# Two-layer kernel on one core: the gate's product ahead of the step's relu, a high part moved from step 10 to step 8 of a segment, and stage B's sums taken through PSUM

## The chip, the cores and the metric

The kernel runs on one core of one Trainium2 chip. The time is device microseconds of one execution, given as the median of several. Besides that, one execution was taken by the hardware profiler; all views below come from it. Engines: PE is TensorE (matmul), DVE is VectorE, ACT is ScalarE, POOL is GpSimd, SP issues the DMAs.

## The reference

The input x has 4 batches of 12608 tokens with 128 channels. First an induced attention with 32 inducing points, then a channel mix with 1024 hidden channels:

```python
def mab(q, kv):
    s = scale * (q @ kv.transpose(0, 2, 1))
    a = np.exp(s - s.max(-1, keepdims=True))
    a /= a.sum(-1, keepdims=True) + 1e-09
    return a @ kv
h = mab(I, x)                 # I: 32 inducing points
x = mab(x, h)                 # every token attends to the 32 rows of h
x_prev = x shifted by one token
xk = mu_k * x + (1.0 - mu_k) * x_prev
xr = mu_r * x + (1.0 - mu_r) * x_prev
k = np.maximum(xk @ w_k, 0.0)
v = k * k @ w_v
r = 1.0 / (1.0 + np.exp(-(xr @ w_r)))
out = r * v
```

## The kernel before

Channels lie on the partitions, tokens in the free dimension. A batch is cut into 25 groups of 512 tokens (the last has 320), and a group's 1024 hidden channels into 4 units of 256. One unit is one **step**; there are 400 steps, numbered n, and every step issues the same skeleton:

- `up`: four matmuls of 512 columns into the PSUM tile `ps_a` (two buffers; lines 773 and 775). The weights W hold h times w_k, so that the second attention's product is folded into them, and R holds the attention weights as a high and a low part.
- `square`: the **relu** on DVE, `ps_a` to `k_t` (line 785); then `kh`, the square rounded to float32r (**high part**), by ACT from `k_t` (line 790) or, in the steps that the set `high_vector` names, by DVE from `ps_a` (line 787); then ACT's full square in place in `k_t` (line 791); then POOL's difference `kl` = `k_t` - `kh` (line 793). `k_t`, `kh` and `kl` have four buffers each.
- in a group's second step, `zgate`: two matmuls (lines 762 and 763) into the bank `ps_v` (two buffers) for the group, and ACT's sigmoid into `rT` (line 765).
- `down` of the step four before: six matmuls (line 804) that sum into the group's `ps_v`.
- one step after a group's last `down`, the **gate**: `oT` = `ps_v` times `rT` on DVE (line 809). It frees the bank that the `zgate` of the next step takes. A step later `store` transposes `oT` into `ot` (line 820), and every fourth group four DMAs write `ot` out.

Beside this run two other stages, put into the steps by numbers written out by hand (`at`: at the end of a step; `soon`: after its `up`). They repeat every 12 steps, a **segment**; steps 0 to 11 below count within it, and the gate falls into steps 0, 4 and 8.

- **Stage A** (of the next batch, so in batches 0 to 2, six segments each): the first attention over a block of 2048 tokens. Step 9 ends with its scores on PE (line 361, into bank a of `pb`) and DVE's maximum (line 364); step 11 has the small matmul `common` (line 371) into bank b of `pb`, and DVE's running maximum; in a batch's last segment `t_scores` (line 349) goes into bank b in step 11 as well. The sum over tokens goes into bank a (line 426), from where `acc` on DVE takes it in step 8 (line 441).
- **Stage B** (all batches): the second attention's weights for a block. Step 1 ends with its scores on PE into bank b (line 610); then on DVE a transpose and the maximum (lines 617, 620), the subtraction (line 623) in step 3, ACT's exponential in step 4, in step 6 the sums over 32 points, the added 1e-9 and the reciprocal (lines 631, 632, 635), in step 7 the product and the transpose back into bank b. ACT copies a rounded high part `ah` in step 8 (line 650), DVE takes the **low part** `al` in step 10 (line 654), which is the last reader of bank b. SP then spreads both into R.

The program keeps the order in which it is written on each engine; each engine runs its own list in order and waits at semaphores.

Of the kernel before, what the change touches and what calls it, by code (L numbers as in the profile page):

```python
# [8 lines left out]
F32 = mybir.dt.float32  # L9
# [4 lines left out]
ALU = mybir.AluOpType  # L14
AX = mybir.AxisListType
EPS = 1e-9
# [3 lines left out]
def kernel(  # L20
# [11 lines left out]
    nc = tc.nc  # L32
# [3 lines left out]
    P = 128  # L36
    Q = 4
# [7 lines left out]
    LAG = 4  # L45
    NU = FC // UC
# [8 lines left out]
    sm = ctx.enter_context(tc.tile_pool(name="sm", bufs=2))  # L55
# [7 lines left out]
    def pb_tile(bank=None):  # L63

        return pb.tile([P, G], F32, name="pb_" + (bank or next(banks)))
# [516 lines left out]
    def halo(S, g, far=True):  # L582

        if g == 0:
            nc.vector.memset(S.R[g].bitcast(F32)[:, 0:1], 0.0)
        elif far:
            nc.sync.dma_start(out=S.R[g].bitcast(F32)[:, 0:1], in_=S.R[g - 1].bitcast(F32)[:, G:G + 1])
        else:
            nc.vector.tensor_copy(out=S.R[g][:, 0:1], in_=S.R[g - 1].bitcast(F32)[:, G:G + 1])


    def stage_b(b, j, at, t):

        S = batches[b]
        full = j < NBLK - 1
        L = {}
        if full:
            w = G  # L600
        else:
            w = (TAIL // Q + 31) // 32 * 32
            offs = [min(i * w, TAIL - w) for i in range(Q)]
        nk = w // 32

        def scores():
            ps = L["ps"] = pb_tile("b")
            for i in range(Q):
                rhs = S.xt[j, i] if full else S.xt_tail[:, offs[i]:offs[i] + w]
                nc.tensor.matmul(out=ps[M * i:M * (i + 1), :w], lhsT=S.hT, rhs=rhs,  # L610
                                 start=True, stop=True)
            for i in range(Q):
                S.xt.pop((j, i))

        def trans():
            L["s2"] = st.tile([P, Q * Q, M], F32, name="s2")[:, :nk, :]
            nc.vector.transpose(out=L["s2"].rearrange("p k m -> p (k m)"), in_=L["ps"][:, :w])

        def maxi():
            nc.vector.tensor_reduce(out=L["ps"][:, :nk], in_=L["s2"], op=ALU.max, axis=AX.X)  # L620

        def sub():
            nc.vector.tensor_tensor(out=L["s2"], in0=L["s2"], op=ALU.subtract,
                                    in1=L["ps"][:, :nk].unsqueeze(2).broadcast_to([P, nk, M]))

        def expo():
            nc.scalar.activation(out=L["s2"], in_=L["s2"], func=AF.Exp, scale=scale)

        def total():
            L["sm"] = sm.tile([P, Q * Q, 2], F32, name="sm3", bufs=1)[:, :nk, 0]  # L630
            nc.vector.tensor_reduce(out=L["sm"], in_=L["s2"], op=ALU.add, axis=AX.X)
            nc.vector.tensor_scalar(out=L["sm"], in0=L["sm"], scalar1=EPS, scalar2=None, op0=ALU.add)  # L632

        def recip():
            nc.vector.reciprocal(out=L["ps"][:, :nk], in_=L["sm"])

        def mult():
            nc.vector.tensor_tensor(out=L["s2"], in0=L["s2"], op=ALU.mult,
                                    in1=L["ps"][:, :nk].unsqueeze(2).broadcast_to([P, nk, M]))

        def back():
            L["aT"] = L["ps"][:, :w]
            if full and b > 0:
                nc.vector.transpose(out=L["aT"].rearrange("p (q s) -> p s q", q=M), in_=L["s2"])
            else:
                nc.vector.transpose(out=L["aT"], in_=L["s2"].rearrange("p k m -> p (k m)"))

        def high():
            L["ah"] = st.tile([P, G], F32R, name="ah")[:, :w]
            nc.scalar.copy(out=L["ah"], in_=L["aT"])  # L650

        def low():
            L["al"] = st.tile([P, G], F32R, name="al")[:, :w]
            nc.vector.tensor_tensor(out=L["al"], in0=L["aT"], in1=L["ah"].bitcast(F32), op=ALU.subtract)

        def spread(i):
            src = (L["ah"].bitcast(F32), L["al"].bitcast(F32))
            if full or i == 0:
                S.R[j * Q + i] = r_pool.tile([P, G + 1], F32R, name="R")
                halo(S, j * Q + i)  # L660
            R = S.R[j * Q + (i if full else 0)].bitcast(F32)
            o, lo = (0, 0) if full else (offs[i], i * w - offs[i])
            for q in range(Q):
                nc.sync.dma_start(out=R[M * q:M * (q + 1), 1 + o + lo:1 + o + w],  # L664
                                  in_=src[q % 2][M * i:M * (i + 1), lo:w])

        at(t, scores)
        at(t + 1, trans)
        at(t + 1, maxi)
        at(t + 2, sub)  # L670
        at(t + 3, expo)
        at(t + 5, total)
        at(t + 5, recip)
        at(t + 6, mult)
        at(t + 6, back)
        at(t + 7, high)
        at(t + 9, low)
        for i in range(Q):
            at(t + 10 + i, lambda i=i: spread(i))
# [154 lines left out]
    def run(th):  # L834
        for f in th:
            f()
# [58 lines left out]
    def head():  # L895


        last = NBLK - 1
        for k in range(2):
            ab[k].tr()  # L900
        ab[0].scores()
        for k in range(NBLK):
            ab[k].maxi()
            ab[k].expo()
            place(PARTS[k][0])
            if k > 0:
                ab[k - 1].hmm()
            if k == last:
                maxes()
            if k > 0:  # L910
                ab[k - 1].acc()
            if k == 0:
                constants()
            if k + 2 < NBLK:
                ab[k + 2].tr()
            place(PARTS[k][1])
            ab[k].etrans()
            ab[k].ecopy()
            ab[k].sums()
            if k < last:  # L920
                ab[k + 1].scores()
            place(PARTS[k][2])
        spin(8)
        weights()
        ab[last].hmm()
        place(PARTS_END)
        ab[last].acc()
        load_x(1, 0)
        hfin()
        place(len(work))  # L930
# [5 lines left out]
    def at(n, f):  # L936
        events.setdefault(n, []).append(f)
# [43 lines left out]
    high_vector = set()  # L981
    for b in range(B):
        t = b * UB + (4 if b == 0 else 0)
        for j in range(NBLK - 1):
            s = t + SEG * j
            high_vector |= {s + 4, s + 10}
            if b + 1 < B:
                stage_a(b + 1, j, at, s)
            stage_b(b, j + 1, at, s + 1)
        if b + 1 < B:  # L990
            s = t + SEG * (NBLK - 1)
            combine(b + 1, at, s)
            stage_b(b + 1, 0, at, s + 13)
    units = []
# [6 lines left out]
    with tc.manual_schedule():  # L1001
        head()
        start()
        for n in range(len(units) + LAG + 2):
            grp, u = units[n] if n < len(units) else (None, n % NU)
            old, ou = units[n - LAG] if LAG <= n < len(units) + LAG else (None, 0)
            if grp is None:
                run(late)
                late = []
            else:  # L1010
                grp.up(u)
                run(early.pop(n, []))
                low = grp.square(u, n in high_vector)
                run(late)
                late = []
                part = grp.w - (grp.w // 2 if n >= len(units) - 3 else 0)
                low(nc.gpsimd, 0, part)
                if part < grp.w:
                    late = [lambda low=low, a=part, z=grp.w: low(nc.vector, a, z)]
                if n == end:  # L1020
                    run(late)
                    late = []
                if n >= NU and u == 1:
                    grp.zgate()
                if u == NU - 2 and n + 2 < len(units):
                    nxt = units[n + 2][0]
                    if nxt.b == 0 and nxt.g < Q:
                        halo(nxt.S, nxt.g, far=False)
            m = n - LAG - 1
            if 0 <= m < len(units) and units[m][1] == NU - 1:  # L1030
                units[m][0].gate()
            if 1 <= m <= len(units) and units[m - 1][1] == NU - 1:
                units[m - 1][0].store()
            if old is not None:
                old.down(ou)
            run(events.pop(n, []))
# [30 lines left out]
```

## Time and profile before

| | before |
|---|---|
| median of 3 runs | 1220.78 us (1220.38 to 1222.27) |
| the profiled execution's own time | 1221.54 us |
| its span, first to last instruction | 1219.7 us |
| PE, DVE, ACT, POOL busy | 92%, 79%, 80%, 78% |
| granted TensorE clock, mean | 0.994 |

Rows of the timeline read: start in us, length in us, engine, line, operation, output<-inputs with their shapes, count, and in brackets the idle time of the engine just before it and what ended it. Rows of waits read: engine, what it wanted to start, whom it waited for, then total us, times, longest us. Rows by line and form read: total busy us, mean ns of one, then idle time before. Rows by windows read: the stretch, its length, then busy us and instruction count of PE, of PE's weight loads, of DVE, ACT and POOL, then the granted clock, the DMA share and GB/s. The start of a row is when the instruction begins; a matmul's length is longer than the distance to the next, since they are pipelined.

### The profile page before, as it was taken

To read this page: it belongs to the slowest core of one execution; us is meant where nothing else is said; L and a number is where in the kernel's file an instruction comes from. 1 tells how busy PE (TensorE), PEld (TensorE's weight loads), DVE (VectorE), ACT (ScalarE), POOL (GpSimd) and SP (SyncE) were. 2 spreads that over 40 slices of the span, in tenths; PEclk is the share of its full clock that TensorE was granted. 3 is DMA by queue.
4 is the path that set the end of the run, shared out by engine and by line. 5 is a ranking of instruction groups with operands and counts; after the bars stand their busy time and mean duration, and the time that the engine had idled before them with its cause. 6 is when DMAs were issued, how large, how long until landed. Compare 5 with 4: busy or idle time off the path is not lost.

```text
span 1219.7 us, 17555 instructions
## 1 busy us (share of the span) xinstructions
PE 1123.6 (92%) x5746; PEld 832.9 (68%) x5746; DVE 964.6 (79%) x1259; ACT 978.6 (80%) x1107; POOL 950.3 (78%) x413
## 2 busy tenths in 40 slices
PE   6768999999998999999999999999999899999998
PEld 5456666666776766666767666666768667767786
DVE  4877888887878888887787788888787787778765
ACT  4577888777887877787988787877789888888996
POOL 1167787887787777787879787878778888889997
PEclk9989999999999999999999999999999999999999
DMA  9112545444225355465034453545304314323222
GB/s 272 50 37 68 117 112 117 88 110 92 37 59 125 102 102 106 107 127 119 6 73 80 103 120 92 117 105 115 52 13 79 60 33 70 70 45 60 41 37 39
DMA packets 273515, 102.31 MB, mean 84 GB/s; under 512 B 232816, under 2 KB 248336, under 8 KB 271120
## 3 DMA queue, kind: packets, MB, share of 16 engines
q1 hardware_dynamic: 273088, 101.17, 38.7%
q8 instruction: 46, 0.75, 0.3%
q14 instruction: 45, 0.37, 0.1%
q10 hardware_dynamic: 336, 0.02, 0.0%
HBM read 28.07 MB, written 25.82 MB: 44 GB/s over the span
## 4 chain that ended last, share of the span: by engine, by line
PE 63%; DVE 21%; issue 5%; DMA 4%; SPq 4%; ACT 2%; DVEq 0%; ACTq 0%
PE ps_v L804 32%; PE ps_a L773 11%; PE ps_a L775 10%; DVE k_t L785 8%; PE ps_v L762 2%; DMA out_dram<-ot 2%; DVE oT L809 2%; PE ps_v L763 2%; PE pb_a L426 2%; DVE kh L787 2%; PE pb_b L610 1%; SPq L664 1%; DVE sm L632 1%; SPq L336 1%; PE pb_a L361 1%
## 5 line engine op out<-in xcount | busy, mean ns | idle before, releaser
L793 POOL TENSOR_TENSOR kl<-k_t,kh 128x1024 fp32r<-128x1024 f32 (+2 forms) x400 | 941.6, 2371 | 220.4 <-ACT k_t L791 191.4
L785 DVE TENSOR_SCALAR k_t<-ps_a 128x1024 f32<-128x1024 f32 (+1 forms) x400 | 480.6, 1202 | 185.8 <-PE ps_a L775 181.6
L791 ACT ACTIVATE k_t<-k_t 128x1024 f32<-128x1024 f32 (+1 forms) x400 | 419.0, 1048 | 77.0 <-DVE kh L787 65.8
L790 ACT ACTIVATE kh<-k_t 128x1024 fp32r<-128x1024 f32 (+1 forms) x352 | 366.9, 1042 | 119.3 <-PE ps_v L804 71.9
L773 PE MATMUL ps_a<-R,W 128*128 128x512 f32 (+1 forms) x800 | 326.8, 409 | 4.1 <-DMA R<-al 3.2
L775 PE MATMUL ps_a<-R,W 128*128 128x512 f32 (+1 forms) x800 | 314.3, 393 | 0.0
L804 PE MATMUL ps_v<-kh,wvh 128*128 128x512 f32 (+1 forms) x800 | 250.7, 395 | 0.1
L804 PE MATMUL ps_v<-kh,wvl 128*128 128x512 f32 (+1 forms) x800 | 249.0, 392 | 0.0
L804 PE MATMUL ps_v<-kl,wvh 128*128 128x512 f32 (+1 forms) x800 | 249.0, 392 | 0.0
L773 PEld LDWEIGHTS ps_a<-R,W 128*128 128x128 f32 x800 | 151.5, 189 | 81.1 <-issue 42.0
L804 PEld LDWEIGHTS ps_v<-kh,wvl 128*128 128x128 f32 x800 | 150.2, 189 | 34.4
L804 PEld LDWEIGHTS ps_v<-kl,wvh 128*128 128x128 f32 x800 | 150.1, 188 | 34.5
L775 PEld LDWEIGHTS ps_a<-R,W 128*128 128x128 f32 x800 | 151.4, 189 | 30.3
L804 PEld LDWEIGHTS ps_v<-kh,wvh 128*128 128x128 f32 x800 | 148.5, 189 | 33.5 <-ACT rT L765 0.8
L762 PE MATMUL ps_v<-R,W 128*128 128x512 f32 (+1 forms) x99 | 42.9, 433 | 41.2 <-DVE oT L809 41.2
L820 DVE STREAM_TRANSPOSE ot<-oT 128x512 f32<-128x512 f32 x96 | 67.2, 700 | 6.8 <-DMA out_dram<-ot 5.9
L809 DVE TENSOR_TENSOR oT<-ps_v,rT 128x512 f32<-128x512 f32 (+1 forms) x100 | 67.0, 670 | 0.5 <-PE ps_v L804 0.5
L787 DVE SCALAR_TENSOR_TENSOR kh<-ps_a,k_t 128x1024 fp32r<-128x1024 f32 x48 | 58.8, 1225 | 5.0
L762 PEld LDWEIGHTS ps_v<-R,W 128*128 128x128 f32 x99 | 18.5, 187 | 63.3 <-DVE oT L809 58.3
L765 ACT ACTIVATE rT<-ps_v 128x512 f32<-128x512 f32 (+1 forms) x99 | 57.3, 579 | 0.3
L333 DVE STREAM_TRANSPOSE xs<-xb 128x512 f32<-128x512 f32 x72 | 50.1, 696 | 0.1
L765 ACT ACT_TABLE_LOAD x31 | 39.8, 1283 | 0.6
(194 smaller groups left out, 694.0 us busy)
## 6 DMA issues: line engine op xcount, KB each, us to landing
out_dram<-ot SPq DMA_DIRECT2D x92, 256.0 KB, 4.4
xb<-in_x_dram SPq DMA_DIRECT2D x18, 1024.0 KB, 5.3
xt<-xs SPq DMA_DIRECT2D x288, 64.0 KB, 2.0
R<-ah SPq DMA_DIRECT2D x184, 64.0 KB, 2.0
R<-al SPq DMA_DIRECT2D x184, 64.0 KB, 2.0
kh<-in_x_dram SPq DMA_DIRECT2D x4, 512.0 KB, 9.0
kl<-in_x_dram SPq DMA_DIRECT2D x4, 512.0 KB, 7.4
xb<-in_x_dram SPq DMA_DIRECT2D x8, 256.0 KB, 5.4
```

What stands on the lines that cost most here:

```text
L762: nc.tensor.matmul(out=ps[:, :w], lhsT=S.W[0][:, F:WF], rhs=R[:, 1:w + 1], start=True, stop=False)
L765: nc.scalar.activation(out=self.rT, in_=ps[:, :w], func=AF.Sigmoid)
L773: nc.tensor.matmul(out=ps[:, c, :w], lhsT=S.W[0][:, cs], rhs=R[:, 1:w + 1], start=True, stop=False)
L775: nc.tensor.matmul(out=ps[:, c, :w], lhsT=S.W[1][:, cs], rhs=R[:, 0:w], start=False, stop=True)
L785: nc.vector.tensor_scalar(out=k, in0=self.ps[:, :, :w], scalar1=0.0, scalar2=None, op0=ALU.max)
L787: nc.vector.scalar_tensor_tensor(out=kh, in0=self.ps[:, :, :w], scalar=0.0, in1=k, op0=ALU.max, op1=ALU.mult)
L790: nc.scalar.activation(out=kh, in_=k, func=AF.Square)
L791: nc.scalar.activation(out=k, in_=k, func=AF.Square)
L793: return lambda eng, a, z: eng.tensor_tensor(out=kl[:, :, a:z], in0=k[:, :, a:z], in1=kh.bitcast(F32)[:, :, a:z], op=ALU.subtract)
L804: nc.tensor.matmul(out=self.v, lhsT=wt[:, fc, :], rhs=kk[:, c, :], start=(fc == 0 and n == 0), stop=(fc == FC - 1 and n == 2))
L809: nc.vector.tensor_tensor(out=self.oT, in0=self.v, in1=self.rT, op=ALU.mult)
L820: nc.vector.transpose(out=ot[:, o:o + w], in_=self.oT)
```

## The change

Three edits. The gate is issued at the head of its step instead of behind `square` and `zgate`, so that it stands ahead of the relu on DVE. In `high_vector`, step 10 of each segment is replaced by step 8; 48 high parts stay on DVE. Stage B's sums are reduced into the first columns of their scores' own PSUM tile, and the addition of 1e-9 reads them there and writes a tile in SBUF (the pool tile `sm2` with two buffers, dense, in place of `sm3` with one, every second column).

```diff
@@ total() of stage_b
-            L["sm"] = sm.tile([P, Q * Q, 2], F32, name="sm3", bufs=1)[:, :nk, 0]
-            nc.vector.tensor_reduce(out=L["sm"], in_=L["s2"], op=ALU.add, axis=AX.X)
-            nc.vector.tensor_scalar(out=L["sm"], in0=L["sm"], scalar1=EPS, scalar2=None, op0=ALU.add)
+            L["sm"] = sm.tile([P, Q * Q], F32, name="sm2")[:, :nk]
+            nc.vector.tensor_reduce(out=L["ps"][:, :nk], in_=L["s2"], op=ALU.add, axis=AX.X)
+            nc.vector.tensor_scalar(out=L["sm"], in0=L["ps"][:, :nk], scalar1=EPS, scalar2=None, op0=ALU.add)
@@ the set of steps with the high part on DVE
-            high_vector |= {s + 4, s + 10}
+            high_vector |= {s + 4, s + 8}
@@ the loop over steps n, at its head
+            m = n - LAG - 1
+            if 0 <= m < len(units) and units[m][1] == NU - 1:
+                units[m][0].gate()
             if grp is None:
...
-            m = n - LAG - 1
-            if 0 <= m < len(units) and units[m][1] == NU - 1:
-                units[m][0].gate()
             if 1 <= m <= len(units) and units[m - 1][1] == NU - 1:
                 units[m - 1][0].store()
```

PE's, POOL's and SP's lists are the same before and after. DVE's list around step 4 of a segment; L623 is stage B's subtraction in step 3, L785 the relu, L787 the high part, L809 the gate, L820 the store's transpose in step 5:

```order
 L623 TENSOR_TENSOR s_1647<-s_1647,pb_b 128x512
-L785 TENSOR_SCALAR k_t<-ps_a 128x1024
-L787 SCALAR_TENSOR_TENSOR kh<-ps_a,k_t 128x1024
-L809 TENSOR_TENSOR oT<-ps_v,rT 128x512
+L809 TENSOR_TENSOR oT<-ps_v,rT 128x512
+L785 TENSOR_SCALAR k_t<-ps_a 128x1024
+L787 SCALAR_TENSOR_TENSOR kh<-ps_a,k_t 128x1024
 L785 TENSOR_SCALAR k_t<-ps_a 128x1024
 L820 STREAM_TRANSPOSE ot<-oT 128x512
```

The gate has moved from behind the relu and the high part of its step to ahead of both. DVE's list of steps 8 to 10 before; L441 is `acc`, L364 the maximum of stage A's scores, L654 the low part:

```order
L785 TENSOR_SCALAR k_t<-ps_a 128x1024
L809 TENSOR_TENSOR oT<-ps_v,rT 128x512
L441 SCALAR_TENSOR_TENSOR acc<-acc,alpha,pb_a 128x128
L785 TENSOR_SCALAR k_t<-ps_a 128x1024
L820 STREAM_TRANSPOSE ot<-oT 128x512
L364 TENSOR_REDUCE mx_1845<-pb_a 128x1
L785 TENSOR_SCALAR k_t<-ps_a 128x1024
L787 SCALAR_TENSOR_TENSOR kh<-ps_a,k_t 128x1024
L654 TENSOR_TENSOR al<-pb_b,ah 128x512
```

And the same steps of the changed kernel on DVE:

```order
L809 TENSOR_TENSOR oT<-ps_v,rT 128x512
L785 TENSOR_SCALAR k_t<-ps_a 128x1024
L787 SCALAR_TENSOR_TENSOR kh<-ps_a,k_t 128x1024
L441 SCALAR_TENSOR_TENSOR acc<-acc,alpha,pb_a 128x128
L785 TENSOR_SCALAR k_t<-ps_a 128x1024
L820 STREAM_TRANSPOSE ot<-oT 128x512
L364 TENSOR_REDUCE mx_1845<-pb_a 128x1
L785 TENSOR_SCALAR k_t<-ps_a 128x1024
L654 TENSOR_TENSOR al<-pb_b,ah 128x512
```

The high part has left its place ahead of the low part in step 10 and stands between the relu and `acc` in step 8, with the gate ahead of all three. On ACT the list changes with it: the square `kh` (line 790) of step 8 goes and that of step 10 comes.

## The prediction

> **What bounds the kernel now.** I read the page's busy shares first, then the table by windows, the waits, and the timeline of one segment.
>
> ```profile
> span 1219.7 us, 17555 instructions
> PE 1123.6 (92%) x5746; PEld 832.9 (68%) x5746; DVE 964.6 (79%) x1259; ACT 978.6 (80%) x1107; POOL 950.3 (78%) x413
> 416.00:560.00 144.00, 135.76 (x708) 98.16 (x707) 122.86 (x160) 116.32 (x129) 115.24 (x49) 1.00 0.50 111
> 960.00:1138.00 178.00, 165.09 (x714) 126.04 (x713) 142.15 (x158) 150.61 (x157) 151.79 (x65) 1.00 0.26 49
> ```
>
> PE is the bound: 92% busy over all and 94% in four segments of batch 1, at a full clock (1.00). The others are under 86% there. So I ask what PE's idle 6% waits for.
>
> ```profile
> DVE k_t L785 <- PE ps_a L775: 181.6, 222, 3.4
> ACT k_t L791 <- DVE kh L787: 65.8, 33, 3.3
> PE ps_v L762 <- DVE oT L809: 41.2, 38, 2.0
> PE pb_b L371 <- DVE al L654: 14.7, 15, 1.0
> DVE ot L820 <- DMA out_dram<-ot: 5.9, 6, 2.2
> PE pb_b L349 <- DVE al L654: 2.7, 3, 1.2
> ```
>
> Nearly all of it is for two DVE instructions: the gate (L809), which frees the ps_v bank that the next gate matmul takes, and the low part (L654), which frees bank b. DVE itself waits 181.6 us for PE, so it is not out of time. It does things in the wrong order, and the timeline shows which:
>
> ```profile
> 502.13 1.22 DVE L785 TENSOR_SCALAR k_t<-ps_a 128x1024 f32<-128x1024 f32 x1 [0.40 <-PE ps_a L775]
> 503.46 1.22 DVE L787 SCALAR_TENSOR_TENSOR kh<-ps_a,k_t 128x1024 fp32r<-128x1024 f32 x1
> 503.97 0.40 PE L775 MATMUL ps_a<-R,W 128*128 128x512 f32 x1
> 504.60 0.68 DVE L654 TENSOR_TENSOR al<-pb_b,ah 128x512 fp32r<-128x512 f32 x1
> 505.33 0.49 PE L371 MATMUL pb_b<-ident,mx 128*128 128x128 f32 x2 [0.96 <-DVE al L654]
> ...
> 518.01 0.40 PE L773 MATMUL ps_a<-R,W 128*128 128x512 f32 x1
> ...
> 519.38 1.21 DVE L785 TENSOR_SCALAR k_t<-ps_a 128x1024 f32<-128x1024 f32 x1
> 520.69 1.23 DVE L787 SCALAR_TENSOR_TENSOR kh<-ps_a,k_t 128x1024 fp32r<-128x1024 f32 x1
> 521.03 0.40 PE L775 MATMUL ps_a<-R,W 128*128 128x512 f32 x1
> 521.83 0.68 DVE L809 TENSOR_TENSOR oT<-ps_v,rT 128x512 f32<-128x512 f32 x1
> 522.43 1.22 DVE L785 TENSOR_SCALAR k_t<-ps_a 128x1024 f32<-128x1024 f32 x1
> 522.57 0.50 PE L762 MATMUL ps_v<-R,W 128*128 128x512 f32 x1 [1.14 <-DVE oT L809]
> 522.91 0.40 PE L763 MATMUL ps_v<-R,W 128*128 128x512 f32 x1
> 523.14 0.63 PE L804 MATMUL ps_v<-kh,wvh 128*128 128x512 f32 x2
> ```
>
> Step 10 (502 us): relu, high part, low part; PE stands from 504.20 for the low part. Step 4 (519 us): relu, high part, gate; PE stands from 521.26 for the gate.
>
> **What a removed wait is worth.** Unhindered matmuls start 0.23 us apart (522.91 to 523.14). The gate matmul starts 522.57 - 521.03 = 1.54 after its forerunner, 1.31 too late, and its successor comes 0.34 behind it, 0.11 too late: 1.42 for a listed idle of 1.14, so 0.28 more per wait. For L371 it is 1.36 - 0.23 = 1.13 for 0.96, so 0.17 more. All gone gives (41.2 + 38 x 0.28) + (14.7 + 15 x 0.17) + (2.7 + 3 x 0.17) = 51.8 + 17.3 + 3.2 = 72.3 us. That is the ceiling; under it PE has hardly anything to wait for.
>
> **Gate in front (one per group, 100).** In step 4 the gate takes the relu's place at 519.38. Its inputs are there: down of step 3 was issued ahead of step 4's up, whose first matmul stands at 518.01. It ends at 520.06, and PE wants the bank at 521.26: the wait goes, with 1.2 us to spare. Behind it the relu and the high part come 0.60 later (the gate's start to the next start, 521.83 to 522.43), so ps_a is free at 521.92 + 0.60 = 522.52. PE asks for it after the gate matmuls (2 x 0.23) and down (6 x 0.23) at about 523.1: 0.6 us to spare. The relu of step 5 starts at 522.43 as before, since the three are only permuted. So PE gains 1.42 us on DVE here, and DVE's later work has that much less slack. In steps 0 and 8 the gate has only the relu ahead of it, and costs 0.60 in front of it at most; where DVE waits for ps_a anyway (222 times) it costs nothing. PE's, POOL's and SP's orders do not change, and SP is passed by nothing.
>
> **High part from step 10 to step 8.** The low part in step 10 starts one relu behind 502.13, at 503.27 (a relu holds DVE 1.14), and ends at 503.95; PE wants bank b at 504.20. The 17.3 and 3.2 us go, by 0.25 us: the tightest cover in this sum, and since this relu itself waits for PE it moves with PE. ACT makes step 10's kh itself where it had waited for DVE's (65.8/33 = 2.0 us a wait), and makes one kh less in step 8, where that wait now stands. The two cover each other: price 0, and if ACT falls behind, the four buffers of kh and kl go first. Who comes behind the high part in step 8 is the accumulator (L441), which frees bank a for step 9's scores (L361):
>
> ```profile
> 526.56 2.40 POOL L793 TENSOR_TENSOR kl<-k_t,kh 128x1024 fp32r<-128x1024 f32 x1 [0.33 <-ACT k_t L791]
> 527.79 1.20 DVE L632 TENSOR_SCALAR sm<-sm 128x16 f32<-128x16 f32 x1
> ...
> 533.10 0.68 DVE L809 TENSOR_TENSOR oT<-ps_v,rT 128x512 f32<-128x512 f32 x1
> 533.70 0.34 DVE L441 SCALAR_TENSOR_TENSOR acc<-acc,alpha,pb_a 128x128 f32<-128x128 f32 x1
> ...
> 535.97 1.07 PE L361 MATMUL pb_a<-xt,indT 128*32 128x512 f32 x8
> ```
> ```profile
> L620 DVE TENSOR_REDUCE pb_b<-s 128x16 f32<-128x512 f32 x23 | 16.0, 694 | 0.8
> L631 DVE TENSOR_REDUCE sm<-s 128x16 f32<-128x512 f32 x23 | 15.5, 675 | 0.0
> L632 DVE TENSOR_SCALAR sm<-sm 128x16 f32<-128x16 f32 x23 | 30.3, 1317 | 0.8
> L632 DVE TENSOR_SCALAR sm<-sm 128x3 f32<-128x3 f32 x4 | 6.1, 1513 | 0.1
> L500 DVE TENSOR_SCALAR rd<-pb_b 128x1 f32<-128x1 f32 x4 | 0.6, 158 | 0.7 <-PE pb_b L498 0.5
> ```
>
> Slack before: 535.97 - 534.04 = 1.93. The high part takes 1.14 of it and PE's lead from step 5 takes 1.42: 0.63 short, unless the next part gives DVE time back.
>
> **Sums in PSUM.** The add of 16 elements (L632) takes 1317 ns, and in this row it ends (528.99) when POOL's subtraction ends (528.96): it is held by it. With its input in PSUM I take 158 ns, L500's, the nearest row in form (a small add out of pb_b); bounds 158 and 1317. The two-sided bound on the reduction (L631) that now writes into pb_b is 675 ns and L620's 694, the maximum of the same shape into pb_b: 0.02 more. Gain on DVE 23 x 1.16 + 4 x 1.36 = 32 us, hidden while DVE waits for PE, but in step 6 the 1.16 turns the 0.63 short into 0.53 to spare. [...]
>
> **Batch 3**, which has no stage A beside it, has two gate waits per segment:
>
> ```profile
> 992.77 0.49 PE L762 MATMUL ps_v<-R,W 128*128 128x512 f32 x1 [0.99 <-DVE oT L809]
> ...
> 998.57 0.60 ACT L765 ACTIVATE rT<-ps_v 128x512 f32<-128x512 f32 x1
> 1000.32 0.63 PE L804 MATMUL ps_v<-kh,wvh 128*128 128x512 f32 x2
> ...
> 1001.34 9.68 POOL L793 TENSOR_TENSOR kl<-k_t,kh 128x1024 fp32r<-128x1024 f32 x4 [1.54 <-ACT k_t L791]
> 1004.35 0.50 PE L762 MATMUL ps_v<-R,W 128*128 128x512 f32 x1 [1.54 <-DVE oT L809]
> ...
> 1026.38 0.50 PE L762 MATMUL ps_v<-R,W 128*128 128x512 f32 x1 [0.98 <-DVE oT L809]
> ```
>
> Both go: 0.99 + 1.54 + 2 x 0.28 = 3.1 of the 33.6 us that a segment takes (992.77 to 1026.38). Next late: the sigmoid (ends 999.17) frees the bank for down at 1000.32, 1.15 ahead; PE's 1.27 us from the first wait uses that up, so some 0.1 to 0.5 comes back. And POOL: a subtraction takes 2.42 (9.68/4), 29.0 for 12, against 30.5 for PE without waits.
>
> **The sum.** Given back: bank a, 0.2 us in each of the 18 segments with stage A (estimate, between 0 and the 0.63 above), 4; the six waits of the store for the output DMA (5.9 us) grow as a segment shortens by 2.5, half a microsecond on PE each, 3; batch 3's sigmoid and POOL, 0.6 in each of its 8 segments (100 steps), 5. So 72 - 12 = 60 us. The profiled execution took 1221.54, 0.76 over the median of the three runs: 1221.5 - 60 - 0.8 = 1161.
>
> **The rivals.**
> 1. *ACT and POOL become batch 3's bound.* POOL stands 26.2 of 178 us there, 4.9 a segment, behind ACT's bursts; if two thirds of it (3.3) stays, a segment cannot go under 29.0 + 3.3 = 32.3, 1.8 over PE's 30.5, and 1.8 x 8 = 14 us return: 1175. Against it: the buffers of kl are four deep, so a late subtraction is not at once a late matmul. In batches 0 to 2 POOL is busy 115.24 of 144 and has room.
> [...]
> 3. *The accumulator blocks the scores.* DVE's step 8 becomes 0.60 + 1.14 + 1.14 + 0.34 = 3.2 us against a step of 10 x 0.23 = 2.3 on PE, and it comes ahead of L361. Each microsecond that L441 is late beyond the slack costs 18 us; it outweighs the ceiling from 72.3/18 = 4.0 us. At 4.5 the time would be 1230. Against it: even in the worst case above it is 0.63 late.
> 4. *DVE is the real bound*, and PE's waits come back at ps_a: no change, 1221. Against it: 122.86 of 144, four segments, is 30.7 of 36, and 29.6 after the change, below the 33.5 that PE needs (36 - 1.42 - 1.13).
>
> **Chances.** Forecast 0.70 (own range 1149, the ceiling, to 1173), first rival 0.17, second 0.05, third 0.04, fourth 0.02, and 0.02 under the ceiling's time. Faster by over 0.2% (about what a measurement of this kernel can tell from no change) 0.94, within 0.2% 0.02, slower 0.04. The range 1147 to 1184 takes in the forecast, the second rival and most of the first.
>
> **What would show it.** Right: L762 and L371 nearly without idle time behind DVE, PE at 96 to 98% of the span, a segment of batch 1 at 33.5 to 34 instead of 36, L632 near 0.16 us, DVE's wait for ps_a smaller. Wrong: new rows of PE waiting for L441 at L361, for L785 or L787 at L773, or for POOL or ACT at L804; L632 still over 1 us; a granted clock under 1.00 at the higher load.

## The result, and the profile after

The changed kernel takes 1168.28 us in the median of four runs (1165.47 to 1170.43), against 1220.58 us of the kernel before, in four runs too: a ratio of 0.9568, with a 95% interval of 0.9545 to 0.9591, or 52 us less. Forecast were 1161, with a range of 1147 to 1184. The profiled execution is the fastest of the four, 1165.47 us with a span of 1163.7 and the highest granted clock (0.996; the other three have 0.991 to 0.994), so between the two profiled executions 56.1 us went.

From the page, from the table by windows (about four segments of batch 1, almost six of batch 3), and from the waits of the changed kernel:

```profile
span 1163.7 us, 17576 instructions
PE 1114.2 (96%) x5746; PEld 834.2 (72%) x5746; DVE 934.3 (80%) x1259; ACT 970.9 (83%) x1107; POOL 947.7 (81%) x413
400.00:533.00 133.00, 132.01 (x681) 96.55 (x680) 115.11 (x157) 111.79 (x126) 111.73 (x48) 1.00 0.53 118
905.00:1085.00 180.00, 178.68 (x788) 138.34 (x788) 145.44 (x172) 160.98 (x171) 165.50 (x72) 1.00 0.32 59
```
```profile
DVE k_t L785 <- PE ps_a L775: 144.1, 175, 3.0
ACT k_t L791 <- DVE kh L787: 34.3, 24, 2.2
DVE ot L820 <- DMA out_dram<-ot: 11.3, 6, 2.7
PE ps_v L804 <- ACT rT L765: 5.0, 7, 1.2
PE pb_b L371 <- DVE mx L370: 4.0, 3, 1.8
PE pb_b L371 <- DVE al L654: 1.9, 2, 1.2
```

PE's 41.2 us of waiting for the gate have no row any more, the 14.7 us for the low part are 1.9, and L349's 2.7 are gone. In both stretches PE is now busy 99% of the time (132.01 of 133 us, 178.68 of 180). What it still waits for is new or grown: the sigmoid, the maximum over a batch's last tokens (the tail, L370; 2.1 before), and, by way of DVE, the output DMA (5.9 before). Step 4 of a segment in the timeline, as it now runs:

```profile
493.48 0.68 DVE L809 TENSOR_TENSOR oT<-ps_v,rT 128x512 f32<-128x512 f32 x1
494.08 1.21 DVE L785 TENSOR_SCALAR k_t<-ps_a 128x1024 f32<-128x1024 f32 x1
495.15 0.39 PE L775 MATMUL ps_a<-R,W 128*128 128x512 f32 x1
495.38 0.39 PE L762 MATMUL ps_v<-R,W 128*128 128x512 f32 x1
495.39 1.22 DVE L787 SCALAR_TENSOR_TENSOR kh<-ps_a,k_t 128x1024 fp32r<-128x1024 f32 x1
```

The gate ends at 494.16, and the gate matmul follows its forerunner after 0.23 us: no wait, 1.2 us to spare, as forecast. By form, the held add:

```profile
L631 DVE TENSOR_REDUCE pb_b<-s 128x16 f32<-128x512 f32 x23 | 15.7, 684 | 1.2 <-ACT s L627 1.2
L632 DVE TENSOR_SCALAR sm<-pb_b 128x16 f32<-128x16 f32 x23 | 4.0, 174 | 0.8
```

The add fell from 1317 to 174 ns, at 9 ns more for the reduction ahead of it (684 against 675).

### The profile page after: what moved, and what is told of

The parts are those of the page before. It is cut to its first block, busy times and chain, and to the rows that moved or that the text cites. A ratio compares the mean times of both kernels' runs of the same rounds, so it can differ in the third digit from the quotient of the medians.

```text
span 1163.7 us, 17576 instructions
## 1 busy us (share of the span) xinstructions
PE 1114.2 (96%) x5746; PEld 834.2 (72%) x5746; DVE 934.3 (80%) x1259; ACT 970.9 (83%) x1107; POOL 947.7 (81%) x413
## 4 chain that ended last, share of the span: by engine, by line
PE 61%; DVE 15%; ACT 8%; SPq 6%; issue 5%; DMA 4%; DVEq 0%; ACTq 0%
PE ps_v L804 31%; PE ps_a L773 11%; PE ps_a L775 10%; DVE k_t L785 5%; SPq L336 2%; DMA out_dram<-ot 2%; ACT kh L790 2%; SPq L827 2%; PE pb_a L426 1%; PE pb_b L610 1%; PE ps_v L762 1%; PE ps_v L763 1%; SPq L664 1%; ACT k_t L791 1%; PE pb_a L361 1%
## 5 line engine op out<-in xcount | busy, mean ns | idle before, releaser
L785 DVE TENSOR_SCALAR k_t<-ps_a 128x1024 f32<-128x1024 f32 (+1 forms) x400 | 480.9, 1202 | 155.5 <-PE ps_a L775 144.1
L791 ACT ACTIVATE k_t<-k_t 128x1024 f32<-128x1024 f32 (+1 forms) x400 | 418.2, 1048 | 45.5 <-DVE kh L787 34.3
L773 PE MATMUL ps_a<-R,W 128*128 128x512 f32 (+1 forms) x800 | 325.9, 408 | 4.7 <-DMA R<-al 3.4
L804 PE MATMUL ps_v<-kh,wvh 128*128 128x512 f32 (+1 forms) x800 | 251.9, 396 | 5.5 <-ACT rT L765 5.0
L804 PE MATMUL ps_v<-kl,wvh 128*128 128x512 f32 (+1 forms) x800 | 249.2, 393 | 0.0
L804 PE MATMUL ps_v<-kh,wvl 128*128 128x512 f32 (+1 forms) x800 | 249.0, 392 | 0.0
L773 PEld LDWEIGHTS ps_a<-R,W 128*128 128x128 f32 x800 | 151.2, 189 | 82.3 <-issue 22.4
L804 PEld LDWEIGHTS ps_v<-kh,wvh 128*128 128x128 f32 x800 | 147.9, 189 | 42.3 <-ACT rT L765 10.1
L804 PEld LDWEIGHTS ps_v<-kl,wvh 128*128 128x128 f32 x800 | 149.6, 188 | 35.5 <-POOL kl L793 0.3
L804 PEld LDWEIGHTS ps_v<-kh,wvl 128*128 128x128 f32 x800 | 149.8, 188 | 34.9
L820 DVE STREAM_TRANSPOSE ot<-oT 128x512 f32<-128x512 f32 x96 | 67.4, 702 | 12.2 <-DMA out_dram<-ot 11.3
L809 DVE TENSOR_TENSOR oT<-ps_v,rT 128x512 f32<-128x512 f32 (+1 forms) x100 | 66.7, 667 | 2.4 <-PE ps_v L804 0.2
L787 DVE SCALAR_TENSOR_TENSOR kh<-ps_a,k_t 128x1024 fp32r<-128x1024 f32 x48 | 58.8, 1225 | 5.4 <-PE ps_v L804 0.5
L765 ACT ACT_TABLE_LOAD x31 | 39.8, 1283 | 0.6
L762 PE MATMUL ps_v<-R,W 128*128 128x512 f32 (+1 forms) x99 | 38.9, 393 | 0.0
L763 PE MATMUL ps_v<-R,W 128*128 128x512 f32 (+1 forms) x99 | 38.7, 391 | 0.0
```

What stands on the lines that cost most here:

```text
L762: nc.tensor.matmul(out=ps[:, :w], lhsT=S.W[0][:, F:WF], rhs=R[:, 1:w + 1], start=True, stop=False)
L765: nc.scalar.activation(out=self.rT, in_=ps[:, :w], func=AF.Sigmoid)
L773: nc.tensor.matmul(out=ps[:, c, :w], lhsT=S.W[0][:, cs], rhs=R[:, 1:w + 1], start=True, stop=False)
L785: nc.vector.tensor_scalar(out=k, in0=self.ps[:, :, :w], scalar1=0.0, scalar2=None, op0=ALU.max)
L787: nc.vector.scalar_tensor_tensor(out=kh, in0=self.ps[:, :, :w], scalar=0.0, in1=k, op0=ALU.max, op1=ALU.mult)
L791: nc.scalar.activation(out=k, in_=k, func=AF.Square)
```

## The experiments

**Each edit by itself, and each pair.** Theory 1 is the prediction's: PE waits for two DVE instructions that stand behind work that could wait, and each edit removes its own wait. Theory 2 is that DVE's time is what counts. First the gate alone (before, with its call moved):

```diff
+            m = n - LAG - 1
+            if 0 <= m < len(units) and units[m][1] == NU - 1:
+                units[m][0].gate()
             if grp is None:
...
-            m = n - LAG - 1
-            if 0 <= m < len(units) and units[m][1] == NU - 1:
-                units[m][0].gate()
```

> The kernel before with only the gate moved to the head of its step; high parts stay in steps 4 and 10, the sums stay in SBUF. Theory 1 (PE waits for two DVE instructions in the wrong place, each edit removes its own wait): the waits of L762 for the gate go except about 0.5 us a segment in batch 3 behind the held add (L632), the 17 us of L371 for the low part stay: 45 to 50 us faster, about 1174. Theory 2 (what counts is the DVE time that the freed add gives back): DVE's list is only permuted, so PE's waits come back at ps_a within the step: under 15 us faster, 1206 or more.

Measured: 1189.35 us, ratio 0.9731 (0.9717 to 0.9746), 32 us faster.

```profile
PE ps_v L762 <- DVE oT L809: 0.5, 1, 0.5
PE pb_b L371 <- DVE al L654: 16.2, 15, 1.8
```

The gate's wait is down to one of 0.5 us and the low part's stays, as theory 1 has it. In most segments of batches 0 to 2 the starts of L361 (stage A's scores, once a segment) are 34.8 us apart instead of 36.15 (1.35, for the 1.42 of the sum), and those of L610 (stage B's scores) in batch 3 are 31.0 apart instead of 33.6. Theory 2 is out: DVE's list is only permuted, and 32 us went. But 45 to 50 were expected; the output DMA (9.7 us of DVE waiting, 5.9 before) and the sigmoid (5.3 us, 8 waits of PE at L804) took part back already here. How much each took was not worked out.

The high part alone:

```diff
-            high_vector |= {s + 4, s + 10}
+            high_vector |= {s + 4, s + 8}
```

> The kernel before with only the high part moved from step 10 to step 8. Theory 1: the 20 us of L371 and L349 for the low part go, but the gate of step 8 now stands behind relu and high part, so about 1.2 us of gate wait appears at step 9 in each of 18 segments and batch 3's wait there grows by 1.1: together near nothing or up to 10 us slower, 1215 to 1231. Theory 2: no DVE time is returned, 1221.

Measured: 1241.45 us, ratio 1.0156 (1.0139 to 1.0173), 20 us slower, twice the most that was expected.

```profile
PE ps_v L762 <- DVE oT L809: 68.5, 53, 3.1
```

The waits for the low part went and waits for the gate came, 15 more of them and 27.3 us more: about 1 us at step 9 of each segment, and up to 3 us in batch 3 and in a batch's first segment, where the gate of step 8 now stands behind the held add, a relu and a high part. By the prediction's own rate that is 27.3 + 15 x 0.28 - 20.5 = 11 us; for most of the other 9 us the section on the hardware has a cause, with an estimate of 8.

The sums alone:

```diff
-            L["sm"] = sm.tile([P, Q * Q, 2], F32, name="sm3", bufs=1)[:, :nk, 0]
-            nc.vector.tensor_reduce(out=L["sm"], in_=L["s2"], op=ALU.add, axis=AX.X)
...
+            L["sm"] = sm.tile([P, Q * Q], F32, name="sm2")[:, :nk]
+            nc.vector.tensor_reduce(out=L["ps"][:, :nk], in_=L["s2"], op=ALU.add, axis=AX.X)
+            nc.vector.tensor_scalar(out=L["sm"], in0=L["ps"][:, :nk], scalar1=EPS, scalar2=None, op0=ALU.add)
```

> The kernel before with only stage B's sums in PSUM. L632 near 0.17 us instead of 1.3. Theory 1: the 32 us of DVE are mostly hidden, only the gate waits at step 9 of batch 3 (1.5 us) and of the first segments shrink: 8 to 14 us faster, 1207 to 1213. Theory 2: most of the 32 us come out, about 1190.

Measured: 1206.14 us, ratio 0.9875 (0.986 to 0.989), 15.7 us faster: just past theory 1, far from theory 2. Segments with stage A stay at 36.2 us; batch 3's go from 33.6 to 31.9, and a batch's first from 36.4 to 34.5.

```profile
PE ps_v L762 <- DVE oT L809: 29.7, 29, 1.9
```

Half of the 32 us of DVE time comes out, in the segments where the held add stood ahead of a late gate; the segments with stage A beside them do not change. The pairs, as the changed kernel without one edit each (without the high part's move, without the sums, without the gate's move):

> The changed kernel without the move of the high part (gate ahead, sums in PSUM, high parts in steps 4 and 10). Theory 1: the gate waits are gone, the waits of L371 and L349 for the low part stay at 15 to 18 of about 1 us: 17 to 20 us over the changed kernel, 1185 to 1189. Rival (the move only shifts load on DVE and ACT): within 5 us of the changed kernel, 1163 to 1173.

> The changed kernel with stage B's sums in SBUF as before (gate ahead, high part in step 8). Theory 1 as the prediction had it: the held add leaves DVE 1.16 us late at step 8, so bank a is late for L361 and a gate wait is left in batch 3: 8 us over the changed kernel, about 1176. If the single edit's gain adds up as it stood alone (15 us): 1183.

> The changed kernel with the gate behind the relu as before (high part in step 8, sums in PSUM). Theory 1: the gate of steps 4 and 8 stands behind relu and high part, so two waits of 1 to 1.4 us a segment stay: 1215 to 1230. If each edit acted by itself (+20 for the high part, -15 for the sums as measured alone): 1226. Rival (DVE's time is what counts): near 1190.

| kernel | median us | to before | ratio (95%) | L361 apart, batch 1 | L610 apart, batch 3 |
|---|---|---|---|---|---|
| gate | 1189.35 | -32.5 | 0.9731 (0.9717 to 0.9746) | 34.8 | 31.0 |
| high part | 1241.45 | +19.6 | 1.0156 (1.0139 to 1.0173) | 36.15 | 34.9 to 36.5 |
| sums | 1206.14 | -15.7 | 0.9875 (0.9860 to 0.9890) | 36.2 | 31.9 |
| gate + sums | 1188.34 | -33.2 | 0.9729 (0.9714 to 0.9743) | 34.8 | 31.0 |
| gate + high part | 1176.80 | -44.8 | 0.9628 (0.9608 to 0.9648) | 34.0 | 31.0 |
| high part + sums | 1217.24 | -4.3 | 0.9967 (0.9957 to 0.9978) | 36.2 | 33.2 |
| all three | 1168.28 | -52.3 | 0.9568 (0.9545 to 0.9591) | 33.55 | 31.0 |

The column "to before" is against the kernel before in the same series of runs, 1220.6 to 1221.8 us; the two last columns are the distances in segments that nothing else lengthens. All three pairs fell into theory 1's ranges (1185 to 1189, about 1176, 1215 to 1230), and the rivals are out. The edits do not add: the high part's move costs 20 us alone, gains 13 once the gate is in place (1189.35 to 1176.80) and 20 once the sums are as well (1188.34 to 1168.28); the sums gain about 1 with the gate and 8.5 with the gate and the high part. One cause of the 8.5 shows in the timeline of the kernel without the sums, in steps 8 and 9:

```profile
448.02 1.22 DVE L787 SCALAR_TENSOR_TENSOR kh<-ps_a,k_t 128x1024 fp32r<-128x1024 f32 x1
...
449.17 0.34 DVE L441 SCALAR_TENSOR_TENSOR acc<-acc,alpha,pb_a 128x128 f32<-128x128 f32 x1
...
449.60 1.07 PE L361 MATMUL pb_a<-xt,indT 128*32 128x512 f32 x8 [0.38 <-PE ps_v L804]
```

The row names PE's own matmul as the releaser, but what ends just ahead of the scores is the accumulator (449.17 + 0.34 = 449.51) behind the moved high part. In 8 of the 12 segments where a sum is taken the scores start 0.1 us behind the accumulator's end; in the changed kernel they start 0.9 to 1.2 us behind it, so there it holds up nothing. That is the wait for bank a, with up to 0.4 us a segment (34.0 against 33.55). Summed over the 15 distances between a batch's scores it is only 2.9 us in the two profiled executions, though. The rest of their difference lies ahead of the first scores (3.5 us) and between the batches (5.1 us). Between batches 0 and 1 the kernel without the sums twice ran at about half pace, as the last section describes (from 287.13 us pairs of matmuls stand 0.85 us apart instead of 0.46, from 356.66 single ones 0.43 instead of 0.23), and the changed kernel did not (its granted clock from 271 to 372 us is 1.00). So bank a is shown as a cause, but not for the whole 8.5 us, and how much of the rest differs from execution to execution is open.

**What holds the add.** Before, but the add reads the dense tile in SBUF that the reduction has just written, and writes PSUM:

```diff
-            L["sm"] = sm.tile([P, Q * Q, 2], F32, name="sm3", bufs=1)[:, :nk, 0]
-            nc.vector.tensor_reduce(out=L["sm"], in_=L["s2"], op=ALU.add, axis=AX.X)
-            nc.vector.tensor_scalar(out=L["sm"], in0=L["sm"], scalar1=EPS, scalar2=None, op0=ALU.add)
+            L["sm"] = L["ps"][:, :nk]
+            s0 = sm.tile([P, Q * Q], F32, name="sm2")[:, :nk]
+            nc.vector.tensor_reduce(out=s0, in_=L["s2"], op=ALU.add, axis=AX.X)
+            nc.vector.tensor_scalar(out=L["sm"], in0=s0, scalar1=EPS, scalar2=None, op0=ALU.add)
```

> The kernel before, but the reduction writes a dense SBUF tile, the add reads that tile as before and writes into PSUM, and the reciprocal runs in place there. [...] If it is held because it reads what the row before it has just written in SBUF: L632 still 1.3 us in the mean. [...]

Its add, which is line 633 there:

```profile
L633 DVE TENSOR_SCALAR pb_b<-sm 128x16 f32<-128x16 f32 x23 | 4.1, 178 | 0.8
```

178 ns, and one run at 1207.37 us, near the 1206.14 of the sums alone. It still reads what was just written, so that is not what held it: with either end in PSUM it is no longer held, at 174 ns with its input there and 178 with its output, against 1317 with both ends in SBUF. Both free forms also differ from the add before in that they do not work in place on every second column; that this was not the cause either is shown by L519 below, which is held (2144 ns, and 342 with its input in PSUM) without being in place or strided.

**What is left to gain.** Three edits on top of the changed kernel, each at one of its remaining waits. The sigmoid ahead of the squares:

```diff
+                if n >= NU and u == 1:
+                    grp.zgate()
                 low = grp.square(u, n in high_vector)
...
-                if n >= NU and u == 1:
-                    grp.zgate()
```

> The changed kernel, and the gate matmuls with their sigmoid are written ahead of the step's squares, so that ACT makes the sigmoid (and its table load) before the two squares of that step; PE's list is the same. If PE's new waits of L804 for the sigmoid (5.0 us in 7, 0.4 more each) are a cost of the change that the sum priced too low: they go, 5 to 8 us under the changed kernel, 1160 to 1163. If they only stand for another lateness, they come back as waits for kl or ps_a: within 2 us of 1168.

Measured: 1168.21 us, ratio 0.9565 (0.9535 to 0.9594), the same as the changed kernel's. (The table loads are in the changed kernel's trace: 31 at the sigmoid's line, 1283 ns each.) PE's waits for the sigmoid are gone, and batch 3's segments take 30.6 us instead of 31.0, but others came, as the second expectation has it:

```profile
PE ps_v L762 <- DVE oT L809: 1.7, 2, 1.2
PE ps_v L804 <- POOL kl L793: 1.2, 1, 1.2
```

The four runs lie between 1164.6 and 1170.9 us, so their median could hardly show a gain of 3 us.

The operations held by POOL, with the tail's maximum (L370) and sum (L418) taking the second value as a scalar operand and the four products of L519 reading PSUM:

```diff
-                nc.vector.tensor_tensor(out=L["mx"], in0=L["mx"], in1=L["mxt"], op=ALU.max)
+                nc.vector.tensor_scalar(out=L["mx"], in0=L["mx"], scalar1=L["mxt"], scalar2=None, op0=ALU.max)
...
-                nc.vector.tensor_tensor(out=S.sum, in0=S.sum, in1=L["sst"], op=ALU.add)
+                nc.vector.tensor_scalar(out=S.sum, in0=S.sum, scalar1=L["sst"], scalar2=None, op0=ALU.add)
...
-                nc.vector.tensor_scalar(out=h4, in0=h, scalar1=mu, scalar2=None, op0=ALU.mult)
+                nc.vector.tensor_scalar(out=h4, in0=ps[:, :P], scalar1=mu, scalar2=None, op0=ALU.mult)
```

> [...] If the held operations are what is left on the path at a batch's last segment and at the seam (L371 waits 4.0 us for L370): these DVE rows fall from 1.5 and 2.4 to under 0.35 us and the time by 5 to 9 us, to 1159 to 1163. If DVE's slack covers them: within 2 us of 1168.

Measured: 1158.20 us, ratio 0.9486 (0.9464 to 0.9509): 10 us under the changed kernel, a little past the first expectation. Two of the rows by form, each in the changed kernel and then here:

```profile
L519 DVE TENSOR_SCALAR h4k<-hT,omuk 128x128 f32<-128x128 f32 x4 | 8.6, 2144 | 0.0
L519 DVE TENSOR_SCALAR h4k<-pb_b,omuk 128x128 f32<-128x128 f32 x4 | 1.4, 342 | 0.0
L370 DVE TENSOR_TENSOR mx<-mx,mx 128x1 f32<-128x1 f32 x3 | 4.4, 1479 | 0.0
L370 DVE TENSOR_SCALAR mx<-mx,mx 128x1 f32<-128x1 f32 x3 | 0.6, 205 | 0.0
```

In the changed kernel one of L519's products ends at 314.16 and the subtraction that POOL runs beside it at 314.07, as it was with the add; one of L370's maxima ends at 829.05 and the subtraction at 829.03. From the last L361 of a batch to the next batch's first L610 the time falls from 48.3, 47.7 and 47.7 us to 46.0, 44.9 and 44.9, 8 of the 10 us. In the kernel before, these stretches took 48.7, 48.4 and 48.0 us: the cost was there already, and is no part of the 72.3 us that the prediction called the ceiling. The output tile in halves (the lines for the weights that are staged in this tile at the start, and for how much one DMA writes, change with it and are left out):

```diff
-            elif g % Q == 0:
+            elif g % 2 == 0:
                 self.S.ot = out_tile()
             ot = self.S.ot
-            o = (g % Q) * G
+            o = (g % 2) * G
...
-        return mp.tile([P, Q * G], F32, name="ot", bufs=1)
+        return mp.tile([P, 2 * G], F32, name="ot", bufs=2)
```

> The changed kernel with the output tile of four groups cut into two of two groups, in the same memory; the output goes in twice as many DMAs of half the size. If DVE's 11.3 us of waiting for the output DMA is what makes single segments 34 to 35.4 us instead of 33.55 (six of them, about 1.2 each): the wait goes and the time falls by 5 to 8 us, 1160 to 1163. If SP's queue cannot take the added DMAs (1.1 us of issue each): waits of PE for R appear, and the time rises.

Measured: 1161.30 us, ratio 0.9511 (0.9492 to 0.9530), 7 us under the changed kernel, as the first expectation has it. There is no row of DVE waiting for the output DMA any more, and all of batch 1's segments, by L361, take 33.2 to 33.6 us. In the changed kernel, the chain that this breaks looks so:

```profile
510.95 0.71 DVE L820 STREAM_TRANSPOSE ot<-oT 128x512 f32<-128x512 f32 x1 [2.35 <-DMA out_dram<-ot]
511.58 0.65 DVE L364 TENSOR_REDUCE mx<-pb_a 128x1 f32<-128x512 f32 x1
512.16 1.21 DVE L785 TENSOR_SCALAR k_t<-ps_a 128x1024 f32<-128x1024 f32 x1
513.29 0.67 DVE L654 TENSOR_TENSOR al<-pb_b,ah 128x512 fp32r<-128x512 f32 x1
...
514.02 0.49 PE L371 MATMUL pb_b<-ident,mx 128*128 128x128 f32 x2 [0.79 <-DVE al L654]
```

The store waits 2.35 us for the tile, and everything behind it on DVE is late, down to the low part, for which PE waits again. Then all three together, and the last two without the first:

> The changed kernel with all three: sigmoid ahead of the squares, nothing of DVE held by POOL, two output tiles. If the three act in different places: the sum of their gains, 15 to 20 us, 1148 to 1153, close to the ceiling's 1149 of the prediction. If one of them covers another: under 12 us, 1156 or more.

> The kernel of all three edits without the sigmoid's move (nothing of DVE held by POOL, two output tiles, sigmoid behind the squares). If the move is worth nothing on the path, as it was by itself (1168.2 against 1168.3): 1148 to 1151, the same as 1149.4. If the sigmoid waits cost their 5.0 + 7 x 0.4 = 8 us once the other two causes are gone: 1155 to 1158. Adding the gains measured alone gives 1168.3 - 10.1 - 7.0 = 1151.

Measured: 1149.44 us for all three, ratio 0.9415 (0.9396 to 0.9435), the fastest kernel here, 18.8 us under the changed one: the gains add, within the first expectation. From its page:

```profile
span 1146.3 us, 17707 instructions
PE 1110.2 (97%) x5746; PEld 836.3 (73%) x5746; DVE 915.0 (80%) x1259; ACT 970.0 (85%) x1107; POOL 947.2 (83%) x413
```

Without the sigmoid's move it takes 1152.66 us, ratio 0.9434 (0.9421 to 0.9448). That is between the two expectations, and the two intervals overlap a little. The traces show where the difference arises: in batches 1 and 2 the second segment, by L610, takes 32.8 and 33.2 us without the move and 31.6 and 31.9 with it, and in batch 3 the second takes 30.8 instead of 29.7 and those behind it 31.0 instead of 30.6, 5 us together in the two profiled executions. So once the other two causes are gone the move is worth 3 us by the medians and 5 by this pair, not the 8 us of its waits.

## Why the prediction was right or wrong, point by point

- **The bound and the reading** (PE, held up by two DVE instructions in the wrong place): shown. The gate alone takes its 41.2 us row to 0.5, and the full change takes L371's row for the low part to 1.9.
- **The rate per wait** (1.42 for the gate, 1.13 for L371): 1.35 by the gate alone (36.15 to 34.8) and, with the sums in place, 34.8 to 33.55 = 1.25 by the high part's move: 2.60 for the 2.55 of the sum. The mechanism and its size are right.
- **The gate's three permuted instructions**: as forecast; no row of PE waiting at L773 for a relu or high part is over 0.4 us.
- **The high part at price 0**: right for ACT, whose wait for it fell from 65.8 to 34.3 us. What the prediction did not say is that the price is 0 only with the gate in front: alone the move costs 20 us.
- **The sums**: 174 ns for 158 forecast, and no longer held. That the add would be free with its input in PSUM no run had shown when the 158 was taken, from L500's row; it was the author's estimate, and the runs showed 174 ns with the input there and 178 with the output. The 8 us expected of taking this edit away and the 8.5 measured agree in part by luck: bank a, at up to 0.4 us a segment, gives some 3 of them, and in batch 3 nothing came (31.0 with and without). The cover, 0.53 us by the sum, is 0.9 to 1.2 in the trace: with the edit, bank a's 4 us that the sum gave back did not arise.
- **The give-backs were mis-sized.** Summed were 4 (bank a) + 3 (output DMA) + 5 (batch 3) = 12; the profiled pair gave back 72.3 - 56.1 = 16.2. The output DMA costs 7, not 3: the step that failed is "half a microsecond on PE each"; single waits of the store reach 2.7 us. Six segments of the changed kernel are 0.4 to 1.8 us longer than with the halved tile, 6.8 together, 1.1 each; before, none of the steady segments with stage A stood out by over 0.4. Batch 3 gave back 0.5 a segment (31.0 for the 30.5 without waits), 4 for the 5 summed. The tail's maximum, held by POOL, grew from 2.1 to 4.0 us and was no term at all. These make 13 of the 16.2; the rest was not located. The sigmoid's waits were foreseen in batch 3's steady segments; those of the steady kind cost 0.4 a segment there (31.0 against 30.6), while the larger ones, to 1.2 us, stand in the first segments of batches, where the prediction had none. With them one of its signs of being wrong did show, a new row of PE waiting for ACT at L804 (5.0 us).
- **The ceiling**: that under it PE "has hardly anything to wait for" was wrong. It counted three rows of waits; the operations held by POOL between the batches cost 8 us besides, and these stretches were as long before the change. That the kernel with all three further edits lands at 1149.44, the ceiling's 1149, is luck: 8 of its 18.8 us come from there, and some of what the ceiling counted is still given back.
- **The profiled execution against the median**: 0.8 us under its own time was taken for the median, as before the change; now it lies 2.8 above, since the profiled execution happens to be the fastest of four. With 16.2 for 12 this makes the 7 us between 1161 and 1168, about half of it this chance.
- **The first rival** (ACT and POOL bind batch 3 at 32.3): batch 3's segments take 31.0. Of the rest, the **second** (the add still held after the change) is refuted by the 174 ns; the **third** (accumulator ahead of the scores) is real as a mechanism, at up to 0.4 us a segment, without the sums; the **fourth** (DVE the real bound) is refuted by the gate alone.

## What to carry to other kernels

When one engine waits for another that has idle time itself, look at what stands ahead of the awaited instruction in that other engine's list, and count its slack at both ends before moving it: the same move of the high part cost 20 us behind the gate's old place and gained 20 with the gate in front and the sums in PSUM. A small operation that takes eight times as long as a like one (1317 against 158 ns here) may be held by something; here its end (528.99 us) beside the end of POOL's subtraction (528.96) told by what. When the waits are gone, others grow with the pace, as those for the single output tile did (5.9 us of DVE's waiting before, 11.3 after). And a ceiling summed from a few rows of waits is only as good as the choice of rows: the held operations between the batches stood in none of those that were counted.

## What the runs showed of the hardware that was not expected

After some waits PE comes back at about half its pace for 3.4 us. In the kernel with the high part alone, the timeline of PE and the window around it:

```profile
979.83 0.50 PE L762 MATMUL ps_v<-R,W 128*128 128x512 f32 x1 [3.06 <-DVE oT L809]
...
980.47 1.05 PE L804 MATMUL ps_v<-kh,wvh 128*128 128x512 f32 x2
981.33 1.05 PE L804 MATMUL ps_v<-kh,wvl 128*128 128x512 f32 x2
982.18 1.05 PE L804 MATMUL ps_v<-kl,wvh 128*128 128x512 f32 x2
983.03 0.63 PE L773 MATMUL ps_a<-R,W 128*128 128x512 f32 x1
...
984.28 0.62 PE L804 MATMUL ps_v<-kh,wvh 128*128 128x512 f32 x2
...
1016.30 0.50 PE L762 MATMUL ps_v<-R,W 128*128 128x512 f32 x1 [2.86 <-DVE oT L809]
...
1016.86 0.62 PE L804 MATMUL ps_v<-kh,wvh 128*128 128x512 f32 x2
1017.32 0.63 PE L804 MATMUL ps_v<-kh,wvl 128*128 128x512 f32 x2
...
1019.19 0.63 PE L804 MATMUL ps_v<-kh,wvh 128*128 128x512 f32 x2
```
```profile
975.00:985.00 10.00, 6.94 (x24) 5.20 (x23) 6.83 (x9) 6.55 (x8) 7.38 (x4) 0.83 0.03 7
```

Pairs of matmuls follow at 0.85 us instead of 0.46, and the granted clock of these 10 us is 0.83. From the gate matmul to the second `down` behind it (979.83 to 984.28) it is 4.45 us, against 2.89 where the pace is full (1016.30 to 1019.19): 1.56 us lost on top of the wait. The wait's length alone does not decide. Behind the wait of 2.86 us at 1016.30 it did not happen (the granted clock from 1015 to 1025 is 1.00), and in the kernel before one of 1.99 us was enough:

```profile
668.58 0.50 PE L762 MATMUL ps_v<-R,W 128*128 128x512 f32 x1 [1.99 <-DVE oT L809]
...
669.77 1.05 PE L804 MATMUL ps_v<-kh,wvl 128*128 128x512 f32 x2
```

There the granted clock is 0.85, 0.50 and 0.79 in the three stretches of 2 us from 668 to 674. By the granted clock there are 7 such stretches between the first 100 us and the last 5 of the kernel with the high part alone (four of them in the 20 us from 660 at 0.91, the 10 us from 680 at 0.84, and the 10 us from 975 and from 1050 at 0.83), and 2 in the kernel before; over each, the clock falls short by 1.7 us in sum, which makes it 3.4 us long at half pace. Five more at 1.56 us are 8 us, an estimate of this case's numbers for the 9 us that the high part's move cost beyond the 11 us of its waits (the granted clock is 0.985 there, 0.994 before); that they are all of it was not shown. Why PE comes back at half pace behind one wait and not behind a longer one was not shown.
